# Two products' halves in one PSUM bank: up products of w1 and w2 taken together, and seven products for all of block 1

## The chip, the cores and the metric

The kernel runs on one core of one Trainium2 chip. The time is device microseconds of one execution of the whole program, as the median over several executions. Beside it stands one profiled execution with a trace of every instruction; its span runs from its first to its last instruction.

## The reference

An attention without softmax (a gated outer-product recurrence, HGRN2) is followed by a multiplicative feed-forward network:

```python
f = 1.0 / (1.0 + np.exp(-f_logit))
for t in range(S):
    state = f[:, :, t, :, None] * state + np.einsum('bhd,bhe->bhde', k[:, :, t], v[:, :, t])
    y[:, :, t] = np.einsum('bhd,bhde->bhe', q[:, :, t], state)
...
x = np.ascontiguousarray(attn_out.transpose(0, 2, 1, 3)).reshape(B * S, H * D)
a = x @ w1
b = x @ w2
h = a * b @ w3
return (h @ w_out).astype(np.float32)
```

There are 4 batches, 8 heads, 768 positions and 48 dimensions a head, so x is 3072 tokens by 384. w1 and w2 are 384 x 1024, w3 is 1024 x 1024, w_out is 1024 x 384. The kernel works in float32; the weights come as float64 and are narrowed on the chip.

## The kernel before

**Attention.** The 3072 tokens are cut into 24 chunks of 128 positions (u = 0 to 23). For each chunk VectorE makes two scans of the gates (L411 and L433) and scales q and k with them (L427, L441), TensorE multiplies pairs (L464), values (L538), the state's part (L557) and the state's update (L571). From the fifth chunk on these four come as one "visit" of TensorE per chunk. ScalarE copies the scores out of PSUM (L588), GpSimd masks them (L594), and VectorE carries the state (L644, L647, L706). A chunk's result goes through DRAM to be turned into `xt`, the columns of x for four chunks.

**Feed-forward.** Four chunks are a block of 512 tokens (`ffn(n)`, n = 0 to 5). w3 @ w_out is folded once into `wc` (L1239), so that a block needs only the up products a = x w1 and b = x w2, their elementwise product (`ab`), and a down product with `wc`. Block 0 makes the up products plainly (`part`): three matmuls of 128 rows for a column block of 128 and one of the weights, then a copy by ScalarE (a) and a multiplication by VectorE (a times b).

In the later blocks they are made by `seven`, a scheme of Strassen and Winograd: tokens are split in two halves of 256 (TH), the columns of a pair (jc and jc + 4) in two, and the 384 rows in a first part of 128 and the rest. Seven products m1 to m7 replace eight. Some operands are sums made before: `w12t` of the weights (L1271), `xs` of x (L854). The seven products need 1, 2, 2, 2, 1, 1 and 2 matmuls of 256 columns (m1 to m7), eleven in all; a plain pair needs twelve. Each accumulates in one of three PSUM banks, X, Y and Z, taken from a pool "f" of four:

- m1, then m2 go to X; after m1, ScalarE copies X to the tile `a` (k1).
- m6, then m7, then m4 go to Y; VectorE adds Y and `a` after m6 (u2, L908) and after m7 (u3, L911), and Y and `a` after m4 (c21).
- m5, then m3 go to Z; VectorE adds Z and u3 before m3 (c22), and Z and u2 after it (c12).

X after m2, and c21, c22 and c12, are the four quarters of the product. `seven(jc, which)` is called once for w1 (which = 0), where they are the quarters of a, and once for w2, where they are those of b, and VectorE multiplies them with a's quarters (L917, L926). Each of the two calls uses half of each of its banks: 256 of 512 columns. The sums u2 and u3 have two buffers each (`ups`), taken in turn. Block 1 makes its first two column pairs by `part`, in halves of 256 tokens, and the other two by `seven`; blocks 2 to 5 make all four by `seven`.

The down product (`down`) is another scheme of seven, with matmuls of 192 columns; its VectorE sums are L1020 (operands) and L1033 to L1071.

**Order.** The order of the instructions is not written out. Every step is a task of a small planner (`Plan`): an engine, an estimated cost, the tasks it depends on, a priority, and what it takes and frees of a pool (`takes`, `frees`). `Plan.order` starts at each turn the task that can start first, by these estimates, the lower priority number first among equals, and the steps are emitted in that order. Each engine then runs its own queue strictly in that order. A change of a cost or a dependency thus moves other instructions too.

After the last visit the weights are read a second time and checked for their range (L1310, L1314 on ScalarE; 34 rounds); the verdict (from L1322) goes by way of DRAM into a register that the last step of the last down product reads.

Of the kernel before, what the change touches and what calls it, by code (L numbers as in the profile page):

```python
# [36 lines left out]
F32 = mybir.dt.float32  # L37
# [3 lines left out]
ALU = mybir.AluOpType  # L41
# [4 lines left out]
P = 128  # L46
# [3 lines left out]
HP = H // 2  # L50
R = 64 + D
# [4 lines left out]
TB = 512  # L56
UB = TB // C
# [7 lines left out]
TH = TB // 2  # L65
KH = KF // 2
# [133 lines left out]
def up_weights(w12, which, kc, jc):  # L200

    return w12[:, which, kc, jc * P : jc * P + P]


def place_of(jc):

    return jc % KH * 2 + jc // KH
# [7 lines left out]
def ranged(ctx, tc, q, k, f_logit, v, w1, w2, w3, w_out, out, ident, w12, wc, left):  # L215

    nc = tc.nc
# [3 lines left out]
    keep = ctx.enter_context(tc.tile_pool(name="keep", bufs=1))  # L221
    loads = ctx.enter_context(tc.tile_pool(name="loads", bufs=3))
    work = ctx.enter_context(tc.tile_pool(name="work", bufs=2))
# [15 lines left out]
    masked = [t.rearrange("p (r h c) -> p r h c", r=2, h=HP) for t in flat]  # L239
    diag = [t[:, 0 : 2 * HP * W].rearrange("p (r h c) -> p r h c", r=2, h=HP) for t in flat]  # L240
    mids = [t[0:R, 2 * HP * W : 2 * HP * W + HP * D].rearrange("p (h d) -> p h d", d=D) for t in flat]
    sb = [keep.tile([R, HP, R], F32, name=f"sb{i}") for i in range(2)]
    lasts = keep.tile([R, NU, HP], F32, name="lasts")
    ysum = keep.tile([R, NU], F32, name="ysum")
    warm = keep.tile([R, 1], F32, name="warm")
# [5 lines left out]
    def at(a, *shape):  # L251
        n = 1
        for m in shape:
            n *= m
        t = place[:, a : a + n]
        return t.rearrange("p (a b) -> p a b", a=shape[0]) if len(shape) == 2 else t
# [6 lines left out]
    w12t = place[:, 0:5120].rearrange("p (w t c) -> p w t c", w=2, t=5)  # L263
    xss = [at(a, 4, TH) for a in (5120, 12864)]
    wct = [at(6144 + KH * DH * i, KH, DH) for i in range(4)]
    ups = {(nm, i): at(a + 2 * TH * i, TH) for nm, a in (("u2", 9216), ("u3", 9216 + TH)) for i in range(2)}
    abs_ = [at(10240 + KH * P * i, KH, P) for i in range(4)]
    early = abp.tile([P, KH, TB], F32, name="ab")[0:R]
    ks += [early[:, 0], early[:, 1]]
# [4 lines left out]
    plan = Plan()  # L274
# [7 lines left out]
    def bank():  # L282

        return ps_f.tile([P, TB], F32, name=f"f{plan.got}")
# [494 lines left out]
    stores, upq, downq = [], [], []  # L779

    def three(out_, lhs, rhs, start=True):

        for i in range(len(lhs)):
            nc.tensor.matmul(  # L784
                out_, lhsT=lhs[i], rhs=rhs[i], start=start and i == 0, stop=i == len(lhs) - 1,
                skip_group_check=True,
            )

    def ffn(n):
        s = blk[n]  # L790
# [8 lines left out]
        def takes_ab(jc, t):  # L799
            i = place_of(jc) // KH  # L800
            if i not in first_ab:
                first_ab[i] = t
                t["takes"].append("ab")
            return t
# [35 lines left out]
        def xs():  # L840
            return xss[n % 2]

        def quarter(kc, half):
            return s["xt"][:, kc, half * TH : half * TH + TH]
# [11 lines left out]
                last = [q[nm] for q in blk[n - 2].get("seven", []) for nm in ("m5", "m6", "m7", "m3")] if i == 0 else []  # L856
                s["S", i] = plan.add("DVE", 0.43, emit, deps + last + w12_sums[-1:] + folds, 100 * n + 30)

        def seven(jc, which):

            if ("S", 0) not in s:
                sums()
            k = len(upq) % 2
            q = {}
            upq.append(q)
            s.setdefault("seven", []).append(q)
            cols = slice(jc * P, jc * P + P)

            def tw(i):
                return w12t[:, which, i, cols]  # L870

            def wt(kc, half):
                return up_weights(w12, which, kc, jc + half * KH)

            def start(nm):
                q[nm] = bank()[:, 0:TH]
                return q[nm]

            def to(tok, half):
                return a_b(jc + half * KH)[:, tok * TH : tok * TH + TH]  # L880

            def m1():
                three(start("X"), [wt(0, 0)], [quarter(0, 0)])

            def k1():
                q["a"] = work.tile([P, TH], F32, name="a")
                nc.scalar.copy(q["a"], q["X"])  # L887

            def m6():
                three(start("Y"), [tw(1)], [xs()[:, 1]])  # L890

            def m5():
                three(start("Z"), [tw(0)], [xs()[:, 0]])

            def m2():
                three(q["X"], [wt(1, 0), wt(2, 0)], [quarter(1, 0), quarter(2, 0)], False)

            def m7():
                three(q["Y"], [tw(2), wt(2, 1)], [xs()[:, 2], quarter(2, 1)], False)

            def m4():
                three(q["Y"], [tw(3), tw(4)], [quarter(1, 1), quarter(2, 1)], False)

            def m3():
                three(q["Z"], [wt(1, 1), wt(2, 1)], [xs()[:, 3], quarter(2, 0)], False)

            def u2():
                nc.vector.tensor_tensor(ups["u2", k], q["Y"], q["a"], ALU.add)  # L908

            def u3():  # L910
                nc.vector.tensor_tensor(ups["u3", k], q["Y"], q["a"], ALU.add)  # L911

            def c11():
                if which == 0:
                    nc.scalar.copy(to(0, 0), q["X"])
                else:
                    nc.vector.tensor_tensor(to(0, 0), q["X"], to(0, 0), ALU.mult)  # L917

            def ended(tok, half, bank_, more):
                def emit():  # L920
                    m = more()
                    nc.vector.tensor_tensor(m if which else to(tok, half), q[bank_], m, ALU.add)  # L922
                return emit

            def times(tok, half, more):
                return lambda: nc.vector.tensor_tensor(to(tok, half), to(tok, half), more(), ALU.mult)  # L926

            def first():
                return q["a"]

            def second():
                return ups["u2", k]

            def third():
                return ups["u3", k]

            n0 = 100 * n + 50 + 2 * jc + which
            one_, two_ = 0.43, 0.86

            def pe(nm, cost, emit, deps, pr, **kw):  # L940
                q[nm] = plan.add("PE", cost, emit, deps, n0 + pr, **kw)

            def dve(nm, emit, deps, pr=-200, **kw):
                q[nm] = plan.add("DVE", 0.43, emit, deps, n0 + pr, **kw)

            def old(n_, *names):
                return [upq[-1 - n_][nm] for nm in names] if len(upq) > n_ else []

            ready = [tk[n * UB + c]["x"] for c in range(UB)]
            begin = takes_ab(jc, plan.add("PE", 0.0, lambda: None, ready + [s["S", 3]] + old(1, "m7"), n0))  # L950
            pe("m1", one_, m1, [begin], 0, takes=["f"])
            q["k1"] = plan.add("ACT", 0.38, k1, [q["m1"]], -200, takes=["a"])
            pe("m6", one_, m6, [q["m1"]], -1, takes=["f"])
            pe("m5", one_, m5, [q["m6"]], -1, takes=["f"])
            dve("u2", u2, [q["k1"], q["m6"]] + old(2, "e12"))
            pe("m2", two_, m2, [q["k1"], q["m6"]], -5)
            if which == 0:
                q["c11"] = plan.add("ACT", 0.38, c11, [q["m2"]], -200, frees=[q["m1"]])
            else:
                dve("c11", c11, [q["m2"]] + old(1, "c11"), frees=[q["m1"]])  # L960
            pe("m7", two_, m7, [q["u2"], q["m2"]], -5)
            dve("u3", u3, [q["m7"]] + old(2, "e22"))
            dve("c22", ended(1, 1, "Z", third), [q["u3"], q["m5"], q["c11"]])
            pe("m4", two_, m4, [q["u3"]], -6)
            dve("c21", ended(1, 0, "Y", first), [q["m4"], q["c11"]], frees=[q["m6"]])
            pe("m3", two_, m3, [q["c22"], q["m4"]], -6)
            dve("c12", ended(0, 1, "Z", second), [q["m3"]], frees=[q["m5"]])
            if which == 1:
                for nm, tok, half, more in (("22", 1, 1, third), ("21", 1, 0, first), ("12", 0, 1, second)):
                    dve("e" + nm, times(tok, half, more), [q["c" + nm]] + old(1, "c" + nm))  # L970
                s["done"][place_of(jc) // KH].extend([q["c11"], q["e22"], q["e21"], q["e12"]])
            else:
                for nm in ("22", "21", "12"):
                    q["e" + nm] = q["c" + nm]
            q["e21"]["frees"].append(q["k1"])
            s["up"] += [q[nm] for nm in ("m1", "m2", "m7", "m4", "m3")]

        if n == 0:
            part(0, 2, range(KH))
            part(2, 4, range(KH))  # L980
            part(0, 4, range(KH, KF))
        else:
            if n == 1:
                for c in range(0, UB, 2):
                    part(c, c + 2, [jc + half * KH for half in range(2) for jc in range(KH // 2)])
            for jc in range(KH // 2 if n == 1 else 0, KH):
                seven(jc, 0)
                seven(jc, 1)

        def down(i):  # L990
            q = {}
# [122 lines left out]
        for i in range(UB // 2):  # L1114
            q = down(i)
# [265 lines left out]
    for t in plan.order():  # L1381
        if t["eng"] == "PE" and t["at"] < FULL:
            n = int((t["at"] - ready_at) / 0.43)
# [381 lines left out]
```

## Time and profile before

| | us |
|---|---|
| median of 6 runs | 476.28 (475.54 to 476.5) |
| the profiled execution | 475.87 |
| its span, first to last instruction | 474.1 |
| first product of `seven` (block 1) starts | 172.97 |
| plain up products of block 1 | 155.27 to 171 |
| last visit of attention starts | 248.4 |
| last matmul ends | 469.77 |

A line of a timeline gives the start, the time from there to the last end, engine, source line, operation, the tiles written and read, shapes, and a count of instructions that were merged. A group's line gives after the bar its busy time, the mean of one in ns, and the idle time of its engine before it with what ended it. PE is the matmul itself, PEld the loading of its stationary operand, DVE VectorE, ACT ScalarE, POOL GpSimd. Each float32 matmul of the program leaves two records of PE in this trace.

### The profile page before, as it was taken

The numbers are of one execution on the slowest core, as the hardware profiler recorded it, in microseconds if no ns is written. First come the engines' busy times: TensorE is split into PE (matmuls) and PEld (weight loads), VectorE is DVE, ScalarE is ACT, GpSimd is POOL, SyncE is SP. The second block draws the span as 40 slices with busy tenths as digits, with TensorE's granted clock in tenths as the row PEclk, the third lists the DMA queues.
The fourth block names the chain that finished last, engine by engine and source line by source line (L and its number), as shares of the span: only waits on it lengthen the run. The fifth ranks groups of instructions, "written<-read, shape, count | busy, mean of one in ns | idle before, by whom it ended". The sixth has DMA issues, their size and how long they took to land.

```text
span 474.1 us, 11502 instructions
## 1 busy us (share of the span) xinstructions
PE 466.7 (98%) x4673; PEld 400.2 (84%) x4673; DVE 354.3 (75%) x689; ACT 174.4 (37%) x422; POOL 65.7 (14%) x88
## 2 busy tenths in 40 slices
PE   8899999999999999999999999999999999999996
PEld 6788756666599888889988889988899888889996
DVE  8999999999999998889945666366754667655541
ACT  3684344432323453333323454444535540110000
POOL 9320000242231342232120000000000000000000
PEclk9999999999999999999999999999999999999999
DMA  6996898462365765354243446553564510000011
GB/s 179 293 389 176 267 356 276 142 169 61 109 175 151 194 189 152 103 138 134 73 110 106 134 133 201 163 169 121 166 200 151 163 45 2 0 1 1 35 59 45
DMA packets 41532, 67.95 MB, mean 143 GB/s; under 512 B 5105, under 2 KB 26610, under 8 KB 40450
## 3 DMA queue, kind: packets, MB, share of 16 engines
q1 hardware_dynamic: 41474, 67.16, 46.5%
q8 instruction: 38, 0.62, 0.6%
q14 instruction: 20, 0.16, 0.1%
HBM read 58.49 MB, written 8.65 MB: 142 GB/s over the span
## 4 chain that ended last, share of the span: by engine, by line
PE 94%; SPq 2%; DMA 2%; POOL 1%; issue 0%; ACT 0%; DVE 0%; POOLq 0%
PE f L784 73%; PE f L1239 9%; PE py L538 3%; PE pa L464 2%; PE pa L571 2%; PE f L478 2%; PE py L557 2%; SPq L377 2%; DMA place<-in_w_dram 2%; PE f L762 1%; PE f L498 0%; PE f L492 0%; SPq L362 0%; PE py L510 0%; PE pa L454 0%
## 5 line engine op out<-in xcount | busy, mean ns | idle before, releaser
L784 PE MATMUL f<-xt,w 128*128 128x256 f32 (+1 forms) x600 | 160.8, 397 | 0.0
L784 PEld LDWEIGHTS f<-xt,w 128*128 128x128 f32 x600 | 112.9, 190 | 23.8 <-issue 10.0
L784 PE MATMUL f<-place 128*128 128x192 f32 (+1 forms) x504 | 112.7, 350 | 0.0
L784 PEld LDWEIGHTS f<-place 128*128 128x128 f32 x504 | 87.6, 190 | 6.1 <-DVE place L908 0.2
L594 POOL TENSOR_SCALAR_AFFINE_SELECT A<-A 64x512 f32<-64x512 f32 (+1 forms) x44 | 41.9, 953 | 100.8 <-ACT A L588 91.6
L1239 PE MATMUL f<-place 128*128 128x384 f32 x128 | 42.4, 487 | 0.0
L887 ACT COPY a<-f 128x256 f32<-128x256 f32 x36 | 13.4, 372 | 66.0 <-PE f L784 57.2
L1239 PEld LDWEIGHTS f<-place 128*128 128x128 f32 x128 | 23.9, 190 | 15.9 <-ACT place L1180 0.2
L784 PE MATMUL f<-xt,place 128*128 128x256 f32 x144 | 37.1, 380 | 0.0
L784 PE MATMUL f<-wc,ab 128*128 128x192 f32 x192 | 35.3, 327 | 0.0
L911 DVE TENSOR_TENSOR place<-f,a 128x256 f32<-128x256 f32 x36 | 15.3, 424 | 23.7 <-PE f L784 23.6
L784 PEld LDWEIGHTS f<-wc,ab 128*128 128x128 f32 x192 | 31.9, 190 | 0.4
L411 DVE TENSOR_TENSOR_SCAN fwd<-gate,floor 112x512 f32<-112x512 f32 x24 | 29.8, 1240 | 1.1 <-ACT gate L403 0.4
L784 PEld LDWEIGHTS f<-xt,place 128*128 128x128 f32 x144 | 27.0, 189 | 3.6
L433 DVE TENSOR_TENSOR_SCAN bwd<-gate,back 112x512 f32<-112x512 f32 x24 | 29.5, 1227 | 0.7
L1314 ACT ACTIVATE A<-A,back 128x512 f32<-128x512 f32 x34 | 26.3, 773 | 0.7
L1180 ACT ACTIVATE place<-place 128x512 f32<-128x512 uint32 (+2 forms) x24 | 21.0, 898 | 10.9 <-DMA place<-in_w_dram 7.7
L1310 ACT ACTIVATE A<-A 128x512 f32<-128x512 f32 x34 | 23.0, 678 | 4.0 <-DMA A<-in_w_dram 2.9
L697 POOL TENSOR_TENSOR G<-lasts,gate 112x4 f32<-112x4 f32 x20 | 13.0, 648 | 78.2 <-ACT lasts L416 62.5
L733 ACT ACTIVATE ys<-py 112x512 f32<-112x512 f32 x20 | 11.9, 597 | 31.0 <-PE py L557 30.9
L784 PE MATMUL f<-place,w 128*128 128x256 f32 x72 | 21.5, 380 | 0.0
L922 DVE TENSOR_TENSOR ab<-f,place 128x256 f32<-128x256 f32 x36 | 15.2, 424 | 7.3 <-PE f L784 6.1
(135 smaller groups left out, 664.1 us busy)
## 6 DMA issues: line engine op xcount, KB each, us to landing
A<-in_w_dram SPq DMA_DIRECT2D x28, 512.0 KB, 3.9
place<-in_w_dram SPq DMA_DIRECT2D x8, 1024.0 KB, 6.0
place<-in_w_dram SPq DMA_DIRECT2D x12, 512.0 KB, 10.2
out_dram<-o SPq DMA_DIRECT2D x24, 192.0 KB, 1.9
q<-in_q_dram SPq DMA_DIRECT2D x46, 96.0 KB, 2.6
vt<-in_v_dram SPq DMA_DIRECT2D x23, 192.0 KB, 2.7
k<-in_k_dram SPq DMA_DIRECT2D x44, 96.0 KB, 2.8
f<-in_f_logit_dram SPq DMA_DIRECT2D x43, 96.0 KB, 3.0
```

The lines of the kernel that those rows point to most:

```text
L411: nc.vector.tensor_tensor_scan(s["P"], gate[u % 2][:, 0:NQ], floor, 0.0, ALU.mult, ALU.max)
L433: nc.vector.tensor_tensor_scan(s["R"][:, ::-1], gate[u % 2][:, NQ:0:-1], back[:, ::-1], 0.0, ALU.mult, ALU.max)
L538: done = nc.tensor.matmul(y_block(u, hp, par, half)[p0 : p0 + w], lhsT=s["v"][half * W : half * W + W, h * D : h * D + w], rhs=s["A"][half ...
L594: nc.gpsimd.affine_select(out=a, in_=a, pattern=pattern, compare_op=ALU.is_ge, fill=0.0, base=0, channel_multiplier=-1,)
L784: nc.tensor.matmul(out_, lhsT=lhs[i], rhs=rhs[i], start=start and i == 0, stop=i == len(lhs) - 1, skip_group_check=True,)
L887: nc.scalar.copy(q["a"], q["X"])
L911: nc.vector.tensor_tensor(ups["u3", k], q["Y"], q["a"], ALU.add)
L922: nc.vector.tensor_tensor(m if which else to(tok, half), q[bank_], m, ALU.add)
L1180: nc.scalar.activation(lo.bitcast(F32), lo, AF.Copy, bias=2.0, scale=2.0**-51)
L1239: nc.tensor.matmul(w3s["p", jc], lhsT=w3s[jc][:, kc * P : kc * P + P], rhs=wos[:, kc], start=(kc == 0), stop=(kc == KF - 1),)
L1310: return lambda: nc.scalar.activation(a, a, AF.Abs, accum_out=sums_[:, i : i + 1])
L1314: return lambda: nc.scalar.activation(a, a, AF.Sign, bias=small, accum_out=counts[:, i : i + 1])
```

## The change

`seven` loses its argument `which` and handles w1 and w2 of a column pair together. The new helper `both_` writes w1's product to the first 256 columns of a bank and w2's to the other 256, so X, Y and Z are used in full. Copies and sums of `a`, u2, u3, c22, c21 and c12 run over 512 columns; the multiplications of a and b (e22, e21, e12) read both halves of one tile and write `ab`. The first quarter is copied (k11, ScalarE) for a, and multiplied (e11, VectorE) with b. u2 and u3 have one buffer of 512 columns each; the first sums `a` are two tiles of their own (`firsts`), whose memory the early state tiles `sb` also use. The costs told to the planner double or rise to match. Block 1 no longer calls `part`.

```diff
-    sb = [keep.tile([R, HP, R], F32, name=f"sb{i}") for i in range(2)]
+    firsts = [keep.tile([P, TB], F32, name=f"a{i}") for i in range(2)]
+    sb = [t[0:R, 0 : HP * R].rearrange("p (h r) -> p h r", r=R) for t in firsts]
...
-    ups = {(nm, i): at(a + 2 * TH * i, TH) for nm, a in (("u2", 9216), ("u3", 9216 + TH)) for i in range(2)}
+    ups = {nm: at(9216 + TB * i, TB) for i, nm in enumerate(("u2", "u3"))}
...
-        def seven(jc, which):
+        def seven(jc):
...
+            def both_(nm, lhs, rhs, start=False):
+
+                if start:
+                    q[nm] = bank()
+                for which in range(2):
+                    for i in range(len(lhs)):
+                        nc.tensor.matmul(
+                            q[nm][:, which * TH : which * TH + TH], lhsT=lhs[i](which), rhs=rhs[i],
+                            start=start and which == 0 and i == 0, stop=i == len(lhs) - 1, skip_group_check=True,
+                        )
...
             def k1():
-                q["a"] = work.tile([P, TH], F32, name="a")
+                q["a"] = firsts[q["no"] % 2]
                 nc.scalar.copy(q["a"], q["X"])
...
+            def u(nm):
+                return lambda: nc.vector.tensor_tensor(ups[nm], q["Y"], q["a"], ALU.add)
+
+            def k11():
+                nc.scalar.copy(to(0, 0), q["X"][:, 0:TH])
+
+            def e11():
+                nc.vector.tensor_tensor(to(0, 0), q["X"][:, TH:TB], to(0, 0), ALU.mult)
...
+            def ended(bank_, more):
+                return lambda: nc.vector.tensor_tensor(more(), q[bank_], more(), ALU.add)
+
+            def times(tok, half, more):
+                return lambda: nc.vector.tensor_tensor(to(tok, half), more()[:, 0:TH], more()[:, TH:TB], ALU.mult)
...
-            one_, two_ = 0.43, 0.86
+            one_, two_ = 0.86, 1.72
...
-            dve("u2", u2, [q["k1"], q["m6"]] + old(2, "e12"))
+            dve("u2", 0.69, u("u2"), [q["k1"], q["m6"]] + old(1, "e12"))
             pe("m2", two_, m2, [q["k1"], q["m6"]], -5)
-            if which == 0:
-                q["c11"] = plan.add("ACT", 0.38, c11, [q["m2"]], -200, frees=[q["m1"]])
-            else:
-                dve("c11", c11, [q["m2"]] + old(1, "c11"), frees=[q["m1"]])
+            q["k11"] = plan.add("ACT", 0.38, k11, [q["m2"]], -200)
+            dve("e11", 0.43, e11, [q["m2"], q["k11"]], frees=[q["m1"]])
             pe("m7", two_, m7, [q["u2"], q["m2"]], -5)
-            dve("u3", u3, [q["m7"]] + old(2, "e22"))
-            dve("c22", ended(1, 1, "Z", third), [q["u3"], q["m5"], q["c11"]])
+            dve("u3", 0.69, u("u3"), [q["m7"]] + old(1, "e22"))
+            dve("c22", 0.69, ended("Z", third), [q["u3"], q["m5"]])
+            dve("e22", 0.43, times(1, 1, third), [q["c22"]])
             pe("m4", two_, m4, [q["u3"]], -6)
-            dve("c21", ended(1, 0, "Y", first), [q["m4"], q["c11"]], frees=[q["m6"]])
+            dve("c21", 0.69, ended("Y", first), [q["m4"]], frees=[q["m6"]])
+            dve("e21", 0.43, times(1, 0, first), [q["c21"]], frees=[q["k1"]])
             pe("m3", two_, m3, [q["c22"], q["m4"]], -6)
-            dve("c12", ended(0, 1, "Z", second), [q["m3"]], frees=[q["m5"]])
...
+            dve("c12", 0.69, ended("Z", second), [q["m3"]], frees=[q["m5"]])
+            dve("e12", 0.43, times(0, 1, second), [q["c12"]])
...
-            if n == 1:
-                for c in range(0, UB, 2):
-                    part(c, c + 2, [jc + half * KH for half in range(2) for jc in range(KH // 2)])
-            for jc in range(KH // 2 if n == 1 else 0, KH):
-                seven(jc, 0)
-                seven(jc, 1)
+            for jc in range(KH):
+                seven(jc)
```

## The prediction

> **What bounds the kernel now.** I read the page first: busy time by engine, the 40 slices, and the chain that ended last. Its lines are:
>
> ```profile
> PE 466.7 (98%) x4673; PEld 400.2 (84%) x4673; DVE 354.3 (75%) x689; ACT 174.4 (37%) x422; POOL 65.7 (14%) x88
> ...
> PE   8899999999999999999999999999999999999996
> ...
> DVE  8999999999999998889945666366754667655541
> ...
> PE 94%; SPq 2%; DMA 2%; POOL 1%; issue 0%; ACT 0%; DVE 0%; POOLq 0%
> ```
>
> TensorE is busy everywhere and carries 94% of the chain; VectorE carries 0%. It is nearly full only up to about 215 us, while attention runs. But a pipelined PE can look busy while it waits, so I asked for the spacing of matmuls. This is the PE timeline inside a stretch of seven products (start, us from the first start to the last end, count):
>
> ```profile
> 305.70 0.59 PE L784 MATMUL f<-xt,w 128*128 128x256 f32 x2
> 306.13 1.03 PE L784 MATMUL f<-place 128*128 128x256 f32 x4
> 306.99 1.03 PE L784 MATMUL f<-xt,w 128*128 128x256 f32 x4
> 307.86 0.59 PE L784 MATMUL f<-place 128*128 128x256 f32 x2
> 308.29 1.03 PE L784 MATMUL f<-xt,w 128*128 128x256 f32 x4
> ```
>
> Starts advance 0.43 us per two records: 0.216 us a slot, the same whether steps follow each other in one bank or not. Each matmul of the program leaves two records (492 matmuls of 256 columns stand in the built program, 984 in the trace), so one costs 2 x 0.216 = 0.432 us. Of 192 columns, eight records take 1.30 us. The chain from 300 us on is one unbroken piece of it, and then the last VectorE sum:
>
> ```profile
> 299.85 169.92 PE f L784 x879
> 469.77 0.02 issue
> 469.80 0.36 DVE o L1071
> ```
>
> Walking every L784 start against its slot, I find one wait from 250 us to the end (0.09 us, at 392 us), and before that only bubbles of about 0.1 us around attention visits. The bound is the number of slots. The page "Perfetto Trace Analysis" of the Trainium skill (section "Identifying the Most-Contended Engine") speaks against reading PE's 98%: it judges headroom by weight-load time, here 84%. By that, only 84% of a removed slot might be won, 1.45 us in place of the 1.73 below; the unbroken 0.216 us spacing decides for the full slot.
>
> **The change, part by part.**
>
> *Products.* Before, column pairs 0 and 1 of block 1 are plain: 4 column blocks x 2 weights x 3 x 2 token halves = 48 matmuls of 256 columns. Seven products take 1+1+1+2+2+2+2 = 11 per pair and weight, 44 for these. The built programs agree: 492 before, 488 after, and every other TensorE count is equal. So 4 x 0.432 = 1.73 us goes, and all of it lies on the bounding engine.
>
> *Sums.* These rows of the groups, shapes kept apart, price them (after the bar: busy us, mean ns of one, idle before):
>
> ```profile
> L926 DVE TENSOR_TENSOR ab<-ab,place 128x256 f32<-128x256 f32 x36 | 15.3, 426 | 1.2
> L922 DVE TENSOR_TENSOR ab<-f,place 128x256 f32<-128x256 f32 x36 | 15.2, 424 | 7.3 <-PE f L784 6.1
> L826 DVE TENSOR_TENSOR ab<-f,ab 128x512 f32<-128x512 f32 x4 | 2.8, 690 | 0.3 <-PE f L784 0.2
> L821 ACT COPY ab<-f 128x512 f32<-128x512 f32 x4 | 2.3, 586 | 8.1 <-PE f L784 8.1
> ```
>
> A pair for both weights had 14 VectorE instructions, 14 x 0.424 = 5.94 us; now five of 512 and four of 256, 5 x 0.69 + 4 x 0.425 = 5.15. Over the kernel: 18 x 5.94 + 8 x 0.42 = 110.3 before, 20 x 5.15 = 103.0 after, 7.3 us less. ScalarE: 18 x 3 x 0.372 + 8 x 0.37 = 23.0 before, 20 x (0.586 + 0.372) = 19.2 after. Both are priced at nothing: neither engine is on the chain. If it were VectorE that ended things, it would be worth up to those 7.3 us; I see no such place.
>
> *Sums with one buffer.* u2 and u3 had two buffers each; now u2 of pair B may only be written after e12 of pair A, which follows c12, which follows A's m3. Behind it m7 of B waits, and behind m7 all of TensorE's queue. In the built order of the steady stretch A's m3 is followed by B's m2 (4 matmuls) and m5 (2), then m7: 12 slots, 2.59 us of cover. The chain under it needs two hand-overs. PE to VectorE: the last eight slots start at 468.30 and end 1.30 later, at 469.60; the reader starts at 469.80, so 0.20 us. VectorE to PE, from the one wait of the trace:
>
> ```profile
> 392.05 0.42 DVE L908 TENSOR_TENSOR place<-f,a 128x256 f32<-128x256 f32 x1
> ...
> 392.51 0.30 PEld L784 LDWEIGHTS f<-place 128*128 128x128 f32 x2 [0.22 <-DVE place L908]
> ```
>
> The sum ends at 392.47, the load that it held back at 392.81: 0.34 us. With 0.035 us between dependent sums (388.85 to 389.31 for one of 0.42) the chain is 0.20 + 0.725 + 0.46 + 0.69 + 0.34 = 2.42 us. It fits with 0.17 us to spare: price 0. In that steady order nothing else of VectorE stands between c12 and u2. One more 256-column sum there (0.34 us of issue) would make 0.17 us of wait; in all 19 hand-overs that is 3.2 us. The other end is a gain of nothing, since PE already has no wait to lose. I take 0, nearer to the worked chain.
>
> *Other waits.* u3 (0.20 + 0.69 + 0.34 = 1.23 us) is covered by m1 and m6 of the next pair (1.73). e11 now waits for ScalarE's k11, so u3 is queued behind it: 0.20 + 0.37 + about 0.1 + 0.42 = 1.1 us after m2 ends, while u3 can't start before m5 and m7 are through, 2.6 us. X is free for the m6 of the next pair after 1.1 us; m5, m7 and m1 stand between, 3.46 us. Y and Z have over 3 us as well. "PSUM — Partial Sum Buffer" of the Trainium skill (section "PSUM bank collisions raise a hardware error") says that two engines may not touch one bank at once, whatever the columns, so that w1's half has to wait for w2's. By that rule a reader is held two matmuls longer, 0.86 us; the covers just named are counted from the end of both halves, so the sum by it is the same.
>
> *Attention's stretch.* These windows run from block 1's first up product to the last visit of attention (us; then PE, PEld, DVE, ACT, POOL busy):
>
> ```profile
> 155.27:217.08 61.81, 61.81 (x1323) 53.85 (x1321) 55.89 (x108) 25.46 (x66) 20.12 (x26) 1.00 0.56 151
> 217.08:248.30 31.22, 31.22 (x520) 29.49 (x516) 23.50 (x47) 8.64 (x24) 6.43 (x9) 1.00 0.39 109
> ```
>
> Block 1's pairs go from 8 x 0.42 + 2 x 5.94 = 15.2 us of VectorE to 4 x 5.15 = 20.6. Those 5.4 us just fill the first window's idle 5.9. The built order answers: between the same two points stand 130 products where there were 104, 26 x 0.432 = 11.2 us more PE work (once 28 products between two visits; the most before was 13). VectorE's 79.4 of 93.0 us grows by 130/22 x 5.15 - (3.4 + 56/22 x 5.94) = 11.9 to 91.3 of 104.3, 88%. Visits come later, products fill the gap; price 0, with 0 to 5 us as bounds (rival below).
>
> *Moved and renamed.* The weight check starts after the last visit, so its end moves from 389.7 to about 401 us; its verdict is read in the last product, at 468: covered by 67 us. The state tiles share memory with the new first sums; their last reader is over before 36 us, the first sum comes at 155. At the end 22 groups of 4 down matmuls (28.6 us) follow the last up product, so its longer last sums are covered. SP's and POOL's queues hold as many instructions as before (530 and 194), so no DMA is added, only their order shifts with the visits.
>
> *Sum.* The profiled execution took 475.87 us, its span is 474.1 and 1.7 lie around it. 475.87 - 1.73 = 474.14. The median of the six runs, 476.28, is 0.41 above that execution, so as a median: 476.28 - 1.73 = 474.55.
>
> **Rivals.** *Hand-over waits (about the same).* The 0.17 us to spare is thin; if the 512-column chain is 0.27 us longer than worked (the row of another 512-column sum is 757 ns, 0.07 more; two of them, and a sum in between at some pairs), 19 x 0.1 = 1.9 us comes back: 476.4. For it: the thin cover. Against: all of its rows are measured, and the before kernel kept PE full with similar covers. *VectorE becomes the bound in attention (slower).* Between 155 and 217 us its queue is in order and holds scans of 1.24 us (L411, L433). If one scan stands ahead of u2 or u3 in each of block 1's four pairs without cover, 4 x 1.24 = 5.0 us of PE waits: 479.5. It is slower than before by over 0.2% once the waits pass 1.73 + 0.95 = 2.7 us. For it: 55.9 of 61.8 us busy already. Against: visits, 2 us of PE work each, stand between most sums and their readers. *The change doesn't do what it says*: excluded for the slots by the count of 488.
>
> **How the numbers follow.** 0.2% (0.95 us) is about what a measurement tells here. Likeliest, 0.77: 474.55, own range 474.0 to 475.2 (the runs spread 1 us). Same, 0.13: 475.3 to 477.2. Slower, 0.10: 477.3 to 480. The range 473.9 to 475.9 holds the first case and some half of the second. Faster 0.77, same 0.13, slower 0.10.
>
> **What would show it.** Right: 976 records of 256 columns, L-line spacing still 0.216 us, waits of PE on VectorE under 0.5 us in all, attention's last visit near 260 us. Wrong: weight loads idle on VectorE's u2 or u3 sums, 0.1 us at each pair or over 1 us between 155 and 215.

## The result and the profile after

The changed kernel takes 474.47 us (median; 473.92 to 478.92), the kernel before 476.27 (475.54 to 478.95). The ratio is 0.9965, with a 95% interval of 0.9957 to 0.9973: 1.7 us faster by the ratio (the medians differ by 1.80), where 474.55 was forecast. The profiled execution took 474.60 us (before 475.87), its span is 472.9 (before 474.1). Some executions of most kernels here, the one before among them, ran at a granted clock of 0.988 to 0.996 instead of 0.997 to 1.0 and took 2 to 5 us longer; the highest values of the ranges are of that kind, and so are the profiles of e2, e10 and e11, of which only slots and waits are read.

Line numbers of the changed kernel differ: L784 has become L785 (plain and down products) and L881 (`both_`, all seven products), u2 and u3 are L915, c22, c21 and c12 L933, their products with a L936, k1 L894, the visits' values L539, the state's part L558. From its page, busy time by engine, two rows of the slices, shares of the chain that ended last, and three groups:

```profile
PE 465.3 (98%) x4665; PEld 399.1 (84%) x4665; DVE 349.5 (74%) x609; ACT 172.2 (36%) x400; POOL 64.0 (14%) x88
...
PE   8999999999999999999999999999999999999996
...
DVE  8999999999999989989995557436673457554641
...
PE 95%; DVE 1%; POOL 1%; SPq 1%; DMA 1%; issue 1%; ACT 0%; POOLq 0%; DVEq 0%; ACTq 0%
...
L881 PE MATMUL f<-xt,w 128*128 128x256 f32 x400 | 103.4, 380 | 0.0
...
L915 DVE TENSOR_TENSOR place<-f,a 128x512 f32<-128x512 f32 x40 | 27.6, 691 | 22.1 <-PE f L881 20.4
...
L933 DVE TENSOR_TENSOR place<-f,place 128x512 f32<-128x512 f32 x40 | 27.6, 691 | 12.4 <-PE f L881 11.8
```

TensorE has 4665 records in place of 4673 and stays full; VectorE is 4.8 us less busy, with 80 instructions fewer, and its full stretch now reaches to about 248 us (21 slices of 11.8 us; before, 20 slices or 237 us). The chain still runs through TensorE. The new 512-column sums take 691 ns, as priced.

PE's timeline of a steady pair, with the VectorE sums beside it. The first two records end the m3 of the pair in front; then come m6 (four records), m2 (eight) and the start of m7. On VectorE stand c12 and e12 (L936) of the pair in front, then u2:

```profile
272.33 0.59 PE L881 MATMUL f<-xt,w 128*128 128x256 f32 x2
...
272.76 1.03 PE L881 MATMUL f<-place 128*128 128x256 f32 x4
272.96 0.69 DVE L933 TENSOR_TENSOR place<-f,place 128x512 f32<-128x512 f32 x1 [0.57 <-PE f L881]
...
273.62 1.89 PE L881 MATMUL f<-xt,w 128*128 128x256 f32 x8
273.69 0.42 DVE L936 TENSOR_TENSOR ab<-place 128x256 f32<-128x256 f32 x1
274.24 0.69 DVE L915 TENSOR_TENSOR place<-f,a 128x512 f32<-128x512 f32 x1
275.13 0.41 PEld L881 LDWEIGHTS f<-place 128*128 128x128 f32 x2
275.35 0.59 PE L881 MATMUL f<-place 128*128 128x256 f32 x2
```

The starts advance by 0.43 for two records, 0.86 for four, 1.73 for eight: still 0.216 us a slot, with no gap at u2 (L915), which ends at 274.93, 0.42 us before m7's matmul.

To see where the 1.2 us of the span came from, the spacing of every two feed-forward matmuls was compared with the slot of its shape (0.216 us for 256 columns, 0.162 for 192, 0.432 for 512, 0.323 for 384). What exceeds it is a wait of PE: short (25 to 150 ns) or long (more). Slots are thus a count of records times a fixed spacing. Left out are about 1.86 us in each kernel where the visits' own matmuls follow, 1.74 us before the first matmul, and differences under 25 ns, so a row adds up to 3.7 us less than its span. Sums in us:

```
                          slots   short waits   long waits   attention and rest   after last start
before                   383.50      1.74          0              80.47                4.70
after                    381.77      1.94          0              80.63                4.80
```

The slots fell by 1.73 us, the forecast term (eight records fewer at an unchanged 0.216); 0.2 went to two more short waits, 0.3 to the rest. Of two profiles of the changed kernel (this one and e12's) the rest differs by 0.3 as well, so that last figure is no more than two executions differ by.

### The profile page after: what moved, and what is told of

It is laid out like the page before. It is cut to its first block, busy times and chain, and to the rows that moved or that the text cites. A ratio compares the mean times of both kernels' runs of the same rounds, so it can differ in the third digit from the quotient of the medians.

```text
span 472.9 us, 11340 instructions
## 1 busy us (share of the span) xinstructions
PE 465.3 (98%) x4665; PEld 399.1 (84%) x4665; DVE 349.5 (74%) x609; ACT 172.2 (36%) x400; POOL 64.0 (14%) x88
## 4 chain that ended last, share of the span: by engine, by line
PE 95%; DVE 1%; POOL 1%; SPq 1%; DMA 1%; issue 1%; ACT 0%; POOLq 0%; DVEq 0%; ACTq 0%
PE f L881 41%; PE f L785 32%; PE f L1230 9%; PE py L539 3%; PE pa L465 2%; PE pa L572 2%; PE f L479 2%; PE py L558 2%; PE f L763 1%; PE f L493 1%; SPq L378 1%; DMA ab<-in_f_logit_dram 1%; PE pa L455 0%; DVE Q L428 0%; PE f L499 0%
## 5 line engine op out<-in xcount | busy, mean ns | idle before, releaser
L881 PE MATMUL f<-xt,w 128*128 128x256 f32 x400 | 103.4, 380 | 0.0
L881 PEld LDWEIGHTS f<-xt,w 128*128 128x128 f32 x400 | 75.4, 190 | 10.1 <-ACT a L894 0.2
L881 PE MATMUL f<-place 128*128 128x256 f32 x240 | 63.2, 380 | 0.0
L785 PE MATMUL f<-place 128*128 128x192 f32 x288 | 51.3, 328 | 0.0
L881 PEld LDWEIGHTS f<-place 128*128 128x128 f32 x240 | 45.2, 190 | 5.9
L785 PEld LDWEIGHTS f<-place 128*128 128x128 f32 x288 | 47.2, 190 | 0.3
L915 DVE TENSOR_TENSOR place<-f,a 128x512 f32<-128x512 f32 x40 | 27.6, 691 | 22.1 <-PE f L881 20.4
L785 PE MATMUL f<-xt,w 128*128 128x256 f32 (+1 forms) x144 | 42.2, 452 | 0.0
L881 PE MATMUL f<-xt,place 128*128 128x256 f32 x160 | 38.0, 380 | 0.0
L785 PEld LDWEIGHTS f<-xt,w 128*128 128x128 f32 x144 | 27.0, 190 | 12.6 <-issue 10.0
L1230 PEld LDWEIGHTS f<-place 128*128 128x128 f32 x128 | 23.9, 190 | 15.9 <-ACT place L1171 0.2
L933 DVE TENSOR_TENSOR place<-f,place 128x512 f32<-128x512 f32 x40 | 27.6, 691 | 12.4 <-PE f L881 11.8
L785 PE MATMUL f<-wc,ab 128*128 128x192 f32 x192 | 35.2, 326 | 0.0
L881 PEld LDWEIGHTS f<-xt,place 128*128 128x128 f32 x160 | 29.9, 190 | 3.8
L785 PEld LDWEIGHTS f<-wc,ab 128*128 128x128 f32 x192 | 32.0, 190 | 0.4
L933 DVE TENSOR_TENSOR a<-f,a 128x512 f32<-128x512 f32 x20 | 13.8, 691 | 18.1 <-PE f L881 18.0
```

What stands on the lines that cost most here:

```text
L785: nc.tensor.matmul(out_, lhsT=lhs[i], rhs=rhs[i], start=start and i == 0, stop=i == len(lhs) - 1, skip_group_check=True,)
L881: nc.tensor.matmul(q[nm][:, which * TH : which * TH + TH], lhsT=lhs[i](which), rhs=rhs[i], start=start and which == 0 and i == 0, stop=i = ...
L915: return lambda: nc.vector.tensor_tensor(ups[nm], q["Y"], q["a"], ALU.add)
L933: return lambda: nc.vector.tensor_tensor(more(), q[bank_], more(), ALU.add)
L1230: nc.tensor.matmul(w3s["p", jc], lhsT=w3s[jc][:, kc * P : kc * P + P], rhs=wos[:, kc], start=(kc == 0), stop=(kc == KF - 1),)
```

## The experiments

The table gives medians, with the ratio to the kernel before and its interval, and the same sums (the kernel before took 476.07 to 476.11 beside them). "Old form" means w1 and w2 one after the other, each in half a bank, as before.

```
kernel                                        us     ratio [95%]               slots   short  long
e1  joint form, block 1 two pairs plain     476.36  1.0008 [0.9982, 1.0033]   383.50   1.65   0.48
e2  joint form, block 1 one pair plain      475.13  0.9978 [0.9952, 1.0004]   382.63   1.31   0
e3  old form, block 1 all seven             476.12  0.9989 [0.9968, 1.0009]   381.77   2.42   1.13
e4  after + 0.18 us sum ahead of u2         474.56  0.9970 [0.9942, 0.9998]   381.77   1.93   0
e5  after + 0.68 us sum ahead of u2         476.68  1.0015 [0.9994, 1.0035]   381.77   3.09   0.44
e6  before + 0.68 us in late visits         477.83  1.0038 [1.0018, 1.0058]   383.50   2.07   1.30
e7  after + 0.68 us in late visits          478.78  1.0057 [1.0039, 1.0075]   381.77   2.50   2.84
e8  after + block 0's last pair by seven    477.09  1.0020 [1.0001, 1.0038]   380.90   2.18   3.12
e9  e3, m2 and m7 planned later             475.85  1.0000 [0.9976, 1.0024]   381.77   2.10   0.59
e10 e3, m2 after m5                         479.85  1.0073 [1.0049, 1.0097]   381.77   2.84   3.03
e11 e3, m2, m7 and m4 planned later         475.86  0.9995 [0.9985, 1.0004]   381.77   2.26   0.97
e12 the changed kernel again                474.29  0.9964 [0.9951, 0.9978]   381.77   1.93   0
```

**e1 and e2: the two parts of the change, one by one.** The joint form stays; block 1 gets two pairs, or one, by `part` again.

```diff
+            plain = 2 if n == 1 else 0
+            for c in range(0, UB if plain else 0, 2):
+                part(c, c + 2, [jc + half * KH for half in range(2) for jc in range(plain)])
-            for jc in range(KH):
+            for jc in range(plain, KH):
                 seven(jc)
```

(with `plain = 1` in e2)

> The joint products with shared banks, but column pairs 0 and 1 of block 1 plain again (492 matmuls of 256 columns, as before). Slots alone (each removed matmul is 0.432 us): no difference from before, 476.3 us, ratio 1.000. Rival, the 512-column sums of VectorE help by themselves: the gain stays, 474.5 to 475.4. Rival, the shared banks cost hidden waits that the plain block pays for: over 477.

> As the changed kernel, but pair 0 of block 1 plain (490 matmuls). Slots alone: 2 x 0.432 = 0.86 us less than before, 475.4 us, half of the change's gain. VectorE's relief: 474.5 as the changed kernel. A gain bound to something else than the count would not fall half way.

With the 492 products of before, the joint form is worth nothing that these runs can tell (476.36 beside 476.09), though VectorE is busy for 342.7 us there, 11.6 less than before. One long wait appears in e1, of 0.48 us at 390.5, where m7 waits for u2. One plain pair less brings 475.13, two 474.47: 1.23 and 0.66 us a pair, 0.95 in the mean, against 0.86 for two products of 0.432. Over both steps the time follows the slots, as long as the form is the joint one. The single steps are not told apart: the intervals of e1 and e2 are over 1 us to either side, and PE's waits move by as much (2.13, 1.31 and 1.94 us).

**e3: the products without the sharing.** The kernel before, with all of block 1 by the old `seven`. This leaves the same 488 up products as the change.

```diff
-            if n == 1:
-                for c in range(0, UB, 2):
-                    part(c, c + 2, [jc + half * KH for half in range(2) for jc in range(KH // 2)])
-            for jc in range(KH // 2 if n == 1 else 0, KH):
+            for jc in range(KH):
                 seven(jc, 0)
                 seven(jc, 1)
```

> The kernel before, w1 and w2 apart with half banks, but block 1 too by seven products in all column pairs (488 matmuls). Slots alone, and VectorE's queue still not the bound: 474.5 us, the whole gain without shared banks. Rival, the shared banks and longer sums were needed to keep VectorE out of the way in attention (14 sums a pair, 5.94 us, in place of nine, 5.15): 475.4 or more, with TensorE waiting on sums between 155 and 215 us.

A miss: 476.12, nothing won, with the slots of the changed kernel. PE's waits are 1.8 us longer than before (3.55 against 1.74) and eat the 1.73. What the weight loads of e3 wait for from 155 us to the end (us in total, times, the longest), and for the changed kernel below:

```profile
PEld f L784 <- ACT a L887: 1.7, 4, 0.4
PEld f L784 <- DVE place L908: 1.1, 3, 0.4
```

```profile
PEld f L881 <- ACT a L894: 0.2, 1, 0.2
```

The loads of e3 wait seven times for k1 (L887) or u2 (L908); those of the changed kernel once. (A load's idle time also holds time in which it had nothing to do; the matmuls lose less, as the sums above count it.) One such place in e3's timeline:

```profile
236.93 0.59 PE L784 MATMUL f<-xt,w 128*128 128x256 f32 x2
...
237.36 0.59 PE L784 MATMUL f<-place 128*128 128x256 f32 x2
237.56 0.37 ACT L887 COPY a<-f 128x256 f32<-128x256 f32 x1 [1.43 <-PE f L784]
...
237.98 0.73 PEld L784 LDWEIGHTS f<-xt,w 128*128 128x128 f32 x4 [0.43 <-ACT a L887]
```

m1 takes two slots from 236.93. Its slots end at 237.36, the copy k1 starts 0.20 later, runs 0.37, and m2's load starts 0.05 after it: 0.62 us. Only m6 stands in between, 0.43 us. So m2 starts 0.19 late, and the slot after it is lengthened by another 0.10, since the loads no longer run ahead. In the built order of e3 exactly four m2 have a single m6 as their cover, and four waits for k1 are in the trace; before, none had less than 0.86 us of products there. At each of the four places the built order has all four banks of the pool in use, so that m5 could not go ahead. "Perfetto Trace Analysis" of the Trainium skill (section "Optimization Strategy") says that a gap repeating on the engine that should be saturated can mean too little PSUM for the next tile; these four places agree with it, though no run here had a fifth bank.

Where the waits lie matters too. Of e3's six long waits only one (161.85 us) is in block 1. The others start m2 or m7 at 237.98, 246.00, 312.04, 368.50 and 408.52, in blocks 2 to 5, which the kernel before makes in the same old form, with no long wait there. So most of what e3 lost, it lost because the order of later steps moved, not in the products that were added; and the rival's place for the waits, 155 to 215 us, was mostly wrong although its time was right.

In the joint form a step of one matmul for each weight lasts 0.86 us, while the two hand-overs around the copy stay as they are and the copy grows by 0.22 only (0.37 to 0.59). One m2 of the changed kernel, too, has a single m6 as cover, with all four banks in use. It costs nearly nothing:

```profile
400.67 1.03 PE L881 MATMUL f<-place 128*128 128x256 f32 x4
400.87 0.59 ACT L894 COPY a<-f 128x512 f32<-128x512 f32 x1 [1.52 <-PE f L881]
401.51 1.59 PEld L881 LDWEIGHTS f<-xt,w 128*128 128x128 f32 x8 [0.21 <-ACT a L894]
401.53 1.75 PE L881 MATMUL f<-xt,w 128*128 128x256 f32 x7
```

The copy ends at 401.46, m6's slots at 401.53: on time. The next slot is longer by 80 ns, the one wait of the changed kernel after 262 us.

**e4 and e5: how much room u2 has.** The changed kernel, with a VectorE sum over 32 or 512 columns that nobody reads ahead of each u2 (177 and 677 ns a piece, 20 times).

```diff
+    def extra(m):
+        nc.vector.tensor_reduce(out=warm, in_=w12[0:R, 0, 0, 0:m], axis=AX.X, op=ALU.max)
...
             def u(nm):
-                return lambda: nc.vector.tensor_tensor(ups[nm], q["Y"], q["a"], ALU.add)
+                def emit():
+                    if nm == "u2":
+                        extra(32)
+                    nc.vector.tensor_tensor(ups[nm], q["Y"], q["a"], ALU.add)
+                return emit
```

> The changed kernel with one small VectorE reduction (32 columns, about 0.1 us) ahead of each u2, in the same order otherwise. The trace of the changed kernel has TensorE's m7 begin 0.41 to 0.44 us after u2 ends at 8 pairs, against a least hand-over of about 0.35. If 0.08 us is all that is spare there: 8 x 0.02 to 0.05, at most 0.4 us more than the changed kernel, 474.5 to 474.9. With the 0.17 us that was forecast: nothing, 474.5. If the spare is nothing already: 0.1 x 20 = 2 us, 476.5.

> The changed kernel with a VectorE reduction of 512 columns (about 0.6 us) ahead of each u2, otherwise in the same order. Spare of 0.08 us at 8 tight pairs and 0.4 to 1.3 at some others: 8 x (0.6 - 0.08) = 4.2 us plus up to 0.5, 478.7 to 479.2. If the spare were the forecast 0.17 us: 8 x 0.43 = 3.4, 477.9. If the hand-over of u2 never ends last: 474.5.

The short one is free (474.56): in its trace u2 still ends 0.41 to 0.44 us before m7's matmul at the nine tight pairs, as without it. From e4's timeline:

```profile
273.94 0.42 DVE L943 TENSOR_TENSOR ab<-place 128x256 f32<-128x256 f32 x1
274.29 0.18 DVE L276 TENSOR_REDUCE warm<-w 112x1 f32<-112x32 f32 x1
274.50 0.69 DVE L921 TENSOR_TENSOR place<-f,a 128x512 f32<-128x512 f32 x1
```

u2 (L921 here) starts 0.56 us after the product in front of it, where the changed kernel has 0.55 (273.69 to 274.24): the sum fits into the pause that VectorE made there. The long one costs 2.2 us (476.68), in none of the three ranges: less than both theories in which u2 ends last, more than the nothing of the third. The pair shown above, in e5 (VectorE and the load from its timeline; then what weight loads wait for from 262 us on):

```profile
274.75 0.42 DVE L943 TENSOR_TENSOR ab<-place 128x256 f32<-128x256 f32 x1
275.09 0.68 DVE L276 TENSOR_REDUCE warm<-w 112x1 f32<-112x512 f32 x1
275.68 0.68 DVE L921 TENSOR_TENSOR place<-f,a 128x512 f32<-128x512 f32 x1
276.42 0.19 PEld L884 LDWEIGHTS f<-place 128*128 128x128 f32 x1 [0.25 <-DVE place L921]
276.42 0.48 PE L884 MATMUL f<-place 128*128 128x256 f32 x1
```

```profile
PEld f L884 <- DVE place L921: 2.3, 9, 0.3
```

u2 ends at 276.36, and the load starts 0.06 later. The m2 before it began at 274.68, eight slots of 0.216, so m7 was due at 276.41: it is on time, and the price is 0.10 us, the lengthened next slot, at each of nine tight pairs, 0.94 in all. The rest lies elsewhere: one wait of 0.44 us at 175.8 us, 0.2 more of short waits, 0.3 in attention. u2 thus has 0.15 us until a short wait appears (load at 275.13, against 274.93 + 0.05) and some 0.35 us until m7 itself is late.

**e6 and e7: VectorE's reserve while attention runs.** The same 0.68 us sum ahead of the first scan of each chunk from u = 10 on (14 times, 9.5 us of VectorE), in the kernel before and in the changed one.

```diff
             s["P"] = one.tile([R, NQ], F32, name="fwd")
+            if u >= 10:
+                extra(512)
```

> The kernel before with a VectorE reduction of 512 columns (about 0.6 us) ahead of the first scan of each chunk from the eleventh on: 14 x 0.6 = 8.4 us of VectorE more in attention's stretch, where 79.4 of 93.0 us are busy. If VectorE has reserve there: at most 1 us more, 476.3 to 477.3. If it is about to become the bound: 3 us or more, 479.

> The changed kernel with the same 14 reductions. Reserve by the sum (91.3 of 104.3 us busy): as much cost as the kernel before has, at most 1 us, 474.5 to 475.5. If the change has spent VectorE's reserve in attention (the slower rival): clearly more than the kernel before pays for the same load, 3 to 8 us, 477.5 to 482.

The kernel before pays 1.74 us (477.83 - 476.09), between e6's two ranges; the changed one pays 4.3 (478.78 - 474.47). Of e7's two theories, that of reserve by the sum missed, and that of spent reserve held. The long waits of e7 are five of 0.2 to 0.85 us between 200 and 235 us, beside one of 0.4 at 139; four of the five end at the transposes of attention (L484 here). What PE's matmuls wait for from 195 to 262 us in e7:

```profile
PE f L484 <- DVE K L447: 1.0, 2, 0.7
PE f L790 <- DVE place L1029: 0.7, 1, 0.7
PE f L484 <- DVE o L1059: 0.5, 1, 0.5
```

All three are VectorE: the scaled k, which comes after the second scan (L447), and sums of the down product. The change did use up reserve there. Busy time by stretch, of the changed kernel (the two windows are those of the prediction, shifted to its last visit: us, then PE, PEld, DVE, ACT, POOL, clock, DMA share, GB/s):

```profile
155.80:217.10 61.30, 61.30 (x1097) 53.67 (x1096) 56.10 (x98) 22.27 (x54) 15.65 (x21) 1.00 0.52 141
217.10:260.20 43.10, 43.10 (x805) 39.61 (x806) 35.22 (x67) 12.21 (x31) 10.17 (x13) 1.00 0.37 97
```

VectorE has 91.3 of 104.4 us. Its idle time there, 13.1 us, is hardly less than before (13.6 of 93.0), yet the same load costs more than twice as much. Why it does is not settled; that the changed kernel without the load pays nothing there is shown by its waits above.

**e8: one step further.** Block 0's last pair by `seven` too, two products fewer.

```diff
-            part(0, 2, range(KH))
-            part(2, 4, range(KH))
-            part(0, 4, range(KH, KF))
+            part(0, 2, range(KH - 1))
+            part(2, 4, range(KH - 1))
+            part(0, 4, range(KH, KF - 1))
+            seven(KH - 1)
```

> The changed kernel with the last column pair of block 0 by seven products too (2 matmuls of 256 columns fewer in all: 24 gone, 22 come). Slots alone: 2 x 0.432 = 0.86 us less than the changed kernel, 473.6 us, ratio to the kernel before 0.9945. Rival: VectorE, 93% busy from 115 to 155 us, gets 5.15 us of sums and 1.7 of operand sums for 1.4 us of products, and TensorE waits: 474.5 or more.

Slower: 477.09. The slots fall by 0.87 as they should, but two waits of 1.49 and 1.63 us come, at 124.2 and 134.5. What PE waits for there (100 to 155 us); VectorE's busy time from 115 to 155 us in e8 and, below, in the changed kernel (third figure after the length); and VectorE's queue ahead of the late u3:

```profile
PE f L479 <- DVE K L442: 1.5, 1, 1.5
PE f L881 <- DVE place L915: 1.3, 1, 1.3
```

```profile
115.00:155.00 40.00, 37.21 (x648) 34.15 (x640) 37.85 (x70) 12.86 (x33) 8.56 (x12) 1.00 0.41 116
```

```profile
115.00:155.00 40.00, 40.00 (x743) 32.94 (x736) 37.57 (x63) 13.92 (x36) 11.70 (x13) 1.00 0.52 140
```

```profile
121.58 0.68 DVE L1012 TENSOR_TENSOR place<-ab 128x512 f32<-128x512 f32 x1
...
122.18 0.34 DVE L645 TENSOR_TENSOR A<-pa,S 112x192 f32<-112x192 f32 x1
...
122.56 0.36 DVE L648 TENSOR_TENSOR S<-pa,A 112x192 f32<-112x192 f32 x1
122.83 0.41 DVE L921 TENSOR_TENSOR ab<-f,ab 128x256 f32<-128x256 f32 x1
123.17 0.35 DVE L707 TENSOR_TENSOR S<-S,G 112x192 f32<-112x192 f32 x1
123.43 0.68 DVE L915 TENSOR_TENSOR place<-f,a 128x512 f32<-128x512 f32 x1
```

The busy share hardly differs (37.85 and 37.57 of 40 us); what stands in front in the queue does. u3 (L915, 123.43) stands behind attention's state sums (L645, L648, L707), and m4 behind u3. The second wait is attention's own: its transposes (L479) wait for the scaled k (L442), which follows the second scan. This is the slower rival in kind, sums queued behind attention on VectorE, one block earlier, though u3 is held by state sums and not by a scan.

**e9, e10 and e11: is it the bank or only the order?** e3's short covers might be an accident of the planner. Three other orders of the old form, all with 488 products: the planner is told to place readers later (e9, e11), or m2 depends on m5 (e10). e12 is the changed kernel beside e11.

```diff
-            pe("m2", two_, m2, [q["k1"], q["m6"]], -5)
+            pe("m2", two_, m2, [q["k1"], q["m6"]], -5, slack=0.5)
...
-            pe("m7", two_, m7, [q["u2"], q["m2"]], -5)
+            pe("m7", two_, m7, [q["u2"], q["m2"]], -5, slack=0.3)
...
-            pe("m4", two_, m4, [q["u3"]], -6)
+            pe("m4", two_, m4, [q["u3"]], -6, slack=0.3)
```

(e11; e9 has 0.4 at m2, 0.3 at m7 and none at m4; e10 has no slack, but `q["m5"]` among m2's dependencies)

> The kernel of the third experiment (w1 and w2 taken one after the other as before, seven products for all of block 1, 488 up matmuls of 256 columns), with one change: the planner is told that m2 can start only 0.4 us, and m7 only 0.3 us, later than it thought. In the order so built no m2 has a single m6 (0.43 us) as its only cover any more (four had, and each waited 0.19 us for ScalarE's k1 and then lost 0.10 in the next slot, 4 x 0.30 = 1.2 us); the shortest covers of m7 stay as they were. Theory that the slots won in the third experiment were given back by those short covers alone, a matter of the order and not of the shared bank: 476.1 - 1.2 = 474.9, of which up to 0.7 (three waits for u2) remains to be had. Rival, that steps of half the length give the planner too little to cover a hand-over in whatever order: other waits take their place, 475.8 to 476.4.

> The same kernel as the third experiment with another change: m2 now also depends on m5, so that m6 and m5 both stand between m1 and m2. In the built order the cover of m2 is then at least 0.86 us (mostly 2.6 or 3.5), that of m7 3.0 us in 26 of 40 and 1.3 in two; two m4 get a cover of only 0.43 us, against a chain of 0.20 + 0.42 + 0.05 = 0.67 us, so 2 x 0.34 = 0.7 us of wait at most. Theory that only the order is needed: 474.4 to 475.1 (all of the 1.73 us won, less those two). Rival, that the shared bank and the double steps are needed: 475.8 to 476.4. Holding a third bank early is the risk: with four banks the next step may have none, and then it is above 476.4.

> The kernel of the third experiment (w1 and w2 one after the other, seven products for all of block 1, 488 up matmuls of 256 columns) with three notes to the planner: m2, m7 and m4 are to be placed 0.5, 0.3 and 0.3 us later after the sum or copy that they need. In the built order no m2 has less than 0.86 us of TensorE work as cover (chain from m1's end to m2: 0.20 + 0.37 + 0.05 = 0.62), m7 has 2.2 us or more in 39 of 40, m4 1.3 us or more in 35 of 40 (0.86 in the rest; chain 0.20 + 0.42 + 0.05 = 0.67). The ninth experiment's last wait, of 0.59 us behind the eleven small sums of the weight verdict, should not come back, since these no longer stand between a u2 and a u3. Theory that the shared bank is not needed for the gain, only an order without short covers: 474.4 to 475.0, as fast as the changed kernel within 0.5 us. Rival, that single-width steps leave waits in any order of this planner: 475.6 or more.

> The changed kernel itself once more, beside the eleventh experiment on the same chip: 474.3 to 474.8.

e9 lost the four waits for k1, as the order said, but gained 0.27 us of the 1.2 expected, which its interval does not tell from nothing; a wait of 0.59 took their place at 406 us. There the eleven small sums of the weight verdict stand ahead of u3 on VectorE's queue; the first and the last of them in e9's timeline, then u3:

```profile
403.80 0.17 DVE L1319 TENSOR_SCALAR back<-back 128x34 f32<-128x34 f32 x1
...
405.45 0.16 DVE L1340 TENSOR_TENSOR good<-good,back 128x1 f32<-128x1 f32 x1
405.53 0.42 DVE L911 TENSOR_TENSOR place<-f,a 128x256 f32<-128x256 f32 x1
```

e11 took that place away as well, and still has three long waits, 0.97 us together, at 173.6, 316.2 and 405.6. What its weight loads wait for from 160 us on:

```profile
PEld f L784 <- DVE place L911: 1.2, 3, 0.6
PEld f L784 <- DVE ab L922: 0.6, 1, 0.6
...
PEld f L784 <- DVE place L908: 0.4, 1, 0.4
```

They have moved from k1 to u3 (L911), c22 (L922) and, once, u2 (L908). e10, with long covers for m2 and m7, is the worst at 479.85: seven long waits of 0.2 to 1.5 us, 3 us in all. So of four orders of the old form, none wins more than 0.3 us of 1.7. e11 and e12, same chip and same products: 475.86 and 474.29, and their intervals do not touch. That no order of the old form could do it is not shown; a search over orders was not made.

## Why the prediction was right, point by point

*Products, 1.73 us: right in size.* 381.77 against 383.50 us of slots, and from e1 over e2 to the changed kernel the time falls by 1.9 us for the same 1.73 of slots. Whether a slot is worth its spacing (1.73 us in all) or 84% of it (1.45), the medians cannot tell: the interval of the ratio is 1.3 to 2.05 us. The traces speak for the full spacing, since the starts stand at 0.216 us before and after. But the step took it for granted that a slot removed from the bounding engine is won. e3 shows that it is not: there the slots go and waits of the same size come.

*Sums, priced at nothing: right for the changed kernel as a whole, incomplete as a step.* The forecast 7.3 us add up lengths; the page's busy time, which counts overlapping instructions once, fell by 4.8. Less work of VectorE is worth nothing by itself (e1, with 11.6 us less: 476.36). What this working left out is that the sharing doubles the length of TensorE's steps while hand-overs keep their length. Neither part alone gains (e1, e3); together they give 1.7 us. That the longer steps save the wait is shown at like places (237 us in e3, 400 us in the changed kernel); that they are what lets the seven products of block 1 pay is argued from these places and from three other orders, and an order of the old form that does as well is not excluded.

*u2 with one buffer, 0.17 us to spare: right to 0.02, by luck.* Two terms were off and nearly cancel. The 0.34 us from VectorE to PE runs to the end of the second of the two loads that the row merges (392.81). But the held load starts 0.04 us (before, 392.51 after 392.47) to 0.06 (e5) after the sum, and a load that isn't held starts 0.22 us ahead of its matmul (275.13 and 275.35): 0.27 in all. The step from e12 to u2, put at 0.46, takes 0.55 (273.69 to 274.24). Measured, 0.15 us are left until a short wait. The twelve slots of cover are m6 and m2, not m2 and m5 as the working had it, of the same length. What lies beyond was mis-sized: not one for one in 19 hand-overs, but 0.10 us at each of nine tight pairs, until some 0.35 us are used up. The hand-over rival's 1.9 us for a chain longer by 0.27 would by e5 have been 0.9, and e4 shows that it did not even begin.

*Other waits, covered: right.* One of 0.08 us after 262 us, for k1, and none for u2 or u3. (In the steady order u3's cover is m5 and the next pair's m1, not m1 and m6; the length is the same.) k1 starts 0.20 us after the second half's slots have ended (400.67 to 400.87), so a reader waits for both halves, as the working counted; since k1 reads both, that does not test the rule on banks.

*Attention's stretch, price 0 and VectorE at 88%: right.* VectorE was nearly full up to 237 us, by the row of slices, and not 215; the sums by windows do not rest on that. 91.3 of 104.4 us is 87.5%; the last visit starts at 260.0 us and ends at 261.4 (forecast near 260):

```profile
261.10 0.40 PE L558 MATMUL py<-Q,A 48*48 48x64 f32 x16
261.43 0.70 PE L881 MATMUL f<-place,w 128*128 128x256 f32 x2
```

The slower rival, one scan ahead of u2 or u3, did not come in the change itself. e7 and e8 show that it was near: 0.68 us more per chunk costs 4.3 us there, and one pair by `seven` in block 0, where VectorE is busier still (37.57 of 40 us), brings waits of 3.1 us.

*Sum: 474.14 forecast for the profiled execution, 474.60 measured; 474.55 and 474.47 for the median.* The 0.46 us between the two for the profile are the 0.2 of short waits and 0.3 around attention and the end. The two profiled executions differ by 1.27 us and the medians by 1.80, so that the median is met to 0.08 is closer than the working can claim.

## What to carry to other kernels

Count a removed matmul as won only together with the covers that it leaves: list, for each product that waits for a copy or a sum, the products standing in between, and compare them with hand-over, copy and hand-over. Look at the whole order, for a saving in one block can open waits in others (e3). Doing two equal chains side by side doubles each cover while the hand-overs stay, so a change that seems to save only the time of idle engines may be what makes the next saving pay. Test each half alone, for the half that gains nothing may be the one that holds the other up.

## What the runs showed of the hardware

From the end of a product's slots to the start of a copy or a sum that reads it: 0.20 us (e3, 237.36 to 237.56; after, 272.76 to 272.96). From the end of a sum or copy to the start of the weight load that waits for it: 0.05 to 0.06 (e3, 237.93 to 237.98; e5, 276.36 to 276.42). A load that is held and so doesn't run ahead costs a further 0.10 us in the next slot, even where its own matmul starts on time (nine times in e5, 104 ns each). On VectorE, an independent sum starts before its neighbour has ended: in e5 the three above start 0.34 and 0.59 us apart at durations of 0.42 and 0.68.
